# Dividing a head pair's output by one vector instruction: interleaved head columns, a free fourth bank and rows of 640

## The chip, the cores and the metric

One core of a Trainium2 chip runs the kernel. The metric is the device time of one execution in microseconds. The engines are named as in the profile: PE (TensorE), DVE (VectorE), ACT (ScalarE), POOL (GpSimd) and SP (the queue that issues most DMAs).

## What is computed

Eight batches of eight attention heads (576 tokens, head width 64) with rotary positions, then a mixture of eight experts that sends each of the 4608 tokens through its best one:

```python
q_rot, k_rot = (rotate(q), rotate(k))
scores = scale * np.matmul(q_rot, k_rot.transpose(0, 1, 3, 2))
attn = softmax(scores)                     # exp(s - max) / (sum + 1e-9)
x = matmul(attn, v) -> rows of 512 (8 heads x 64)
e_idx = np.argmax(x @ w_gate, axis=1)
out[mask] = gate_w * eom * (relu(x @ w1[e]) @ w2[e])   # for each expert e
```

## The kernel before

**Attention.** A unit of work is a pair of heads; there are 32 pairs (8 batches of 4). A pair's 1152 query rows are taken in nine units of 128. For each unit PE makes the scores (`Pair.score`, L493), DVE takes the row maximum (`peak`, L498), ACT the exponential and its sum (`exp`, L507) and DVE turns it in blocks of 32 (`turn`, L513). PE multiplies with the values (`values`, L535) into `acc`, four banks of PSUM that exist once, so that a pair's first matmul of L535 has to wait until the pair before is done with them. ACT copies `acc` to `ac` (`evict`, L542 to L544). Five matmuls (`back`, L553) turn it back to tokens by rows, each against `ii`, an identity of 128 columns with 32 gate columns behind it, so that 160 columns come out per chunk of 128 tokens: 128 outputs and 2 x 16 gate and output-gate logits. DVE divides by the sums of the softmax while it copies to `xb` (`divide`, L560 to L568). POOL applies the rotary tables for later pairs (`mult`, `add`: L437, L441), splits k and q (`kl`, `ql`: L419) and adds up the sums (`den0`, L516).

**Routing.** Once a batch is divided, `place` adds the logits of its eight heads (`s0`), finds each token's expert, its rank among the tokens of the expert (`rk`, by two matmuls, L685 and L686) and enters it in the experts' lists (`ls`, five matmuls, L729). Both take columns 192 and up of banks 2 and 1 of the `acc` of a later pair. In the last batch these steps run on DVE, in the others on POOL. `store` writes the rows of `xb` to `xd` in DRAM.

**Experts.** From about 545 us on, rows of `xd` are gathered by the lists (`gather`, L1025), transposed (L1055) and multiplied with the weights (L1090 and L1132), which are split in two parts by ACT (L1047) and DVE or POOL (L1049).

The order of all instructions is written by hand: `EVENTS`, `PREP` and the list at the end of `place` give each step a slot relative to the unit at which its pair starts, and each engine takes its instructions in that order. `back` and `divide` of a pair stand in slot 19, when the scores of two pairs later are being made.

Of the kernel before, what the change touches and what calls it, by code (L numbers as in the profile page):

```python
# [10 lines left out]
F32 = mybir.dt.float32  # L11
# [16 lines left out]
NCH = 5  # L28
XW = DM + 1

HL = 2 * E
RW = DM + H * HL

BW = P + 2 * HL
BIG = float(1 << 22)
SLOT = 256

# [2 lines left out]
WHOLE = 1.5 * 2.0 ** 23  # L40


NB, TAIL, PE_, PO = S // 32, 160, 192, 0

EVENTS = [
# [80 lines left out]
def body(ctx, tc, nb, offs, qk, v, rope, cst, gates, w, out):  # L126
    nc = tc.nc
    NT = nb * S

    def pool(st, n, b, **k):  # L130
# [39 lines left out]
    nc.vector.memset(zero, 0.0)  # L170
    nc.scalar.dma_start(out=ct, in_=cst[:, 0:o])
    nc.scalar.dma_start(out=stage[:, 0:nst], in_=cst[:, o:])
    nc.scalar.dma_start(out=ii[:, :, P:].rearrange("p n (h x) -> p n h x", h=2), in_=gates)


    nc.gpsimd.memset(cnt, 0.0)
    nc.gpsimd.memset(lists, 0.0)
    consts = [
        (11, lambda: nc.scalar.copy(ii[:, :, 0:P], ident.unsqueeze(1).broadcast_to((P, NP, P)))),
        (15, lambda: nc.scalar.copy(trib, sc(C_TRI))),  # L180
        (16, lambda: nc.scalar.copy(oneb, sc(C_ONE))),
        (18, lambda: nc.scalar.copy(row, sc(C_ROW))),
# [60 lines left out]
class Attention:  # L243


    def __init__(self, tc, nb, pools, cc, ident, ii, first, trib, oneb, cnt, zero, qk, v, xd, row, lists):
# [27 lines left out]
        xbs = {}  # L274

        def newxb(b):
            xbs[b] = px2.tile([P, NCH, RW], F32, tag="xb", name=f"xb{b}")

            nc.gpsimd.memset(xbs[b][QR:P, NCH - 1, DM:], 0.0)

        for n, pr in enumerate(self.pairs):
            g, b = 9 * n, n // NP
# [79 lines left out]
class Pair:  # L362
# [182 lines left out]

    def back(self):

        parts = []
        for c in range(NCH):
            o = PO if c < 4 else PO + BW  # L550
            parts.append((self.acc[:, c % 4, o:o + BW], self.ac[:, c, :, :].rearrange("p a x -> p (a x)")))
        for out, x in parts:
            self.nc.tensor.matmul(out, x, self.ii[:, self.hp, :], start=True, stop=True, skip_group_check=True)  # L553

    def divide(self, xb):
        nc, V, acc, rz = self.nc, self.nc.vector, self.acc, self.rz
        heads = lambda a, x: a.rearrange("p c (h x) -> p c h x", x=x)
        r4 = rz[:, 0:8].rearrange("p (c h) -> p c h", h=2).unsqueeze(3)
        x0, l0 = self.hp * P, DM + self.hp * 2 * HL
        V.tensor_tensor(out=heads(xb[:, 0:4, x0:x0 + P], D), in0=heads(acc[:, :, PO:PO + P], D),  # L560
                        in1=r4.broadcast_to((P, 4, 2, D)), op=ALU.mult)
        V.tensor_tensor(out=heads(xb[:, 0:4, l0:l0 + 2 * HL], HL), in0=heads(acc[:, :, PO + P:PO + BW], HL),
                        in1=r4.broadcast_to((P, 4, 2, HL)), op=ALU.mult)
        last = acc[0:QR, 0, PO + BW:PO + 2 * BW]
        V.tensor_tensor(out=xb[0:QR, 4, l0:l0 + 2 * HL].rearrange("p (h x) -> p h x", x=HL),
                        in0=last[:, P:BW].rearrange("p (h x) -> p h x", x=HL),
                        in1=rz[0:QR, 8:10].unsqueeze(2).broadcast_to((QR, 2, HL)), op=ALU.mult)
        V.tensor_tensor(out=xb[0:QR, 4, x0:x0 + P].rearrange("p (h x) -> p h x", x=D),  # L568
                        in0=last[:, 0:P].rearrange("p (h x) -> p h x", x=D),
                        in1=rz[0:QR, 8:10].unsqueeze(2).broadcast_to((QR, 2, D)), op=ALU.mult)  # L570
# [8 lines left out]
def place(tc, pools, pairs, b, NT, cc, trib, oneb, cnt, xbs, xd, row, lists):  # L579
# [15 lines left out]
    LO, LG = slice(0, E), slice(E, 2 * E)  # L595

    def s0():
        if not last:

            x = xbs[b][:, :, DM:]  # L600
            h1, h2 = new("h1", [P, NCH, 64]), new("h2", [P, NCH, 32])
            tt(out=h1, in0=x[:, :, 0:64], in1=x[:, :, 64:], op=ALU.add)
            tt(out=h2, in0=h1[:, :, 0:32], in1=h1[:, :, 32:], op=ALU.add)
            tt(out=new("lgs", [P, NCH, 16]), in0=h2[:, :, 0:16], in1=h2[:, :, 16:], op=ALU.add)
            return
        nc.vector.tensor_reduce(new("lgs", [P, NCH, 16]), xbs[b][:, :, DM:].rearrange("p c (h x) -> p c x h", x=HL), axis=AX.X, op=ALU.add)

    def s1():
        nc.vector.tensor_reduce(new("mx", [P, NCH]), T["lgs"][:, :, LO], axis=AX.X, op=ALU.max)
# [153 lines left out]
class Moe:  # L763
# [288 lines left out]
    def turned_in(self, s, h):  # L1052
        tp = self.tps[s, h] = self.small.tile(f"mtp{s}_{h}{self.nm}")
        for dc in range(4):
            self.nc.tensor.transpose(out=tp[:, dc, :], in_=self.xgs[s % 2][:, h, dc * P:dc * P + P], identity=self.ident)  # L1055

    def turn(self, s, h):
        nc, V = self.nc, self.nc.vector
        if s >= self.end or h >= self.todo[s][0]:
            return  # L1060
        if h == 0:
            self.xt[s] = [self.buf(f"xt{i}", 0, 1, 1, [P, 4, SLOT], F32R, f"xt{i}_{s}{self.nm}") for i in range(2)]
            self.gss[s] = self.buf("gs", s, 2, 2, [P, 2], F32, f"gs{s}{self.nm}")
            V.tensor_copy(self.gss[s], self.xgs[s % 2][:, :, DM])
# [149 lines left out]
def layouts(q, k, v, wgt, wog, w1, w2):  # L1214
# [41 lines left out]
```

## Time and profile before

| | us |
|---|---|
| median of 3 runs | 1046.92 |
| lowest and highest run | 1043.89, 1053.6 |
| the profiled execution | 1044.68 |
| its span, first to last instruction | 1042.8 |
| PE busy in it | 969.2 |
| DVE busy in it | 818.0 |
| ACT, POOL busy in it | 616.8, 599.6 |

The span lies 1.9 us below the execution's own time. An engine's busy time says how full it is, not whether it sets the end: in this profile PE is full in the expert part, and the attention part is shared by PE, DVE and POOL, each waiting for one of the others at some place of every pair.

### The profile page before, as it was taken

To read this page: it belongs to the slowest core of one execution; us is meant where nothing else is said; L and a number is where in the kernel's file an instruction comes from. 1 tells how busy PE (TensorE), PEld (TensorE's weight loads), DVE (VectorE), ACT (ScalarE), POOL (GpSimd) and SP (SyncE) were. 2 spreads that over 40 slices of the span, in tenths; PEclk is the share of its full clock that TensorE was granted. 3 is DMA by queue.
4 is the path that set the end of the run, shared out by engine and by line. 5 is a ranking of instruction groups with operands and counts; after the bars stand their busy time and mean duration, and the time that the engine had idled before them with its cause. 6 is when DMAs were issued, how large, how long until landed. Compare 5 with 4: busy or idle time off the path is not lost.

```text
span 1042.8 us, 34822 instructions
## 1 busy us (share of the span) xinstructions
PE 969.2 (93%) x14461; PEld 844.4 (81%) x14461; DVE 818.0 (78%) x1371; ACT 616.8 (59%) x1283; POOL 599.6 (57%) x613
## 2 busy tenths in 40 slices
PE   4999999989999999999799999999999999999995
PEld 4778777767878777777678899998889988899984
DVE  6889989979988898998768777667776867857772
ACT  4656656656655566665445455557766765857762
POOL 4777898887988879889640122206343443443621
PEclk9999999999999999999999999999999999999998
DMA  6665664666745657465548966767886977977860
GB/s 218 164 173 130 179 195 128 177 163 167 198 125 163 185 159 205 118 179 147 160 140 299 300 211 201 230 201 254 312 299 216 356 243 268 325 283 257 299 240 29
DMA packets 58209, 216.32 MB, mean 207 GB/s; under 512 B 9351, under 2 KB 9660, under 8 KB 53952
## 3 DMA queue, kind: packets, MB, share of 16 engines
q1 hardware_dynamic: 50304, 194.03, 59.9%
q0 software_dynamic: 6464, 18.92, 5.0%
q8 instruction: 115, 1.88, 0.8%
q10 hardware_dynamic: 1280, 1.11, 0.3%
q14 instruction: 46, 0.38, 0.1%
HBM read 196.04 MB, written 20.09 MB: 207 GB/s over the span
## 4 chain that ended last, share of the span: by engine, by line
PE 60%; DVE 13%; POOL 10%; issue 8%; ACT 6%; DMA 1%; ACTq 0%; POOLq 0%; DVEq 0%
PE py L1132 17%; PE ph L1090 14%; PE sc L493 11%; PE acc L535 9%; DVE m L498 5%; POOL raw L437 4%; PE ph L1082 4%; ACT pm L507 4%; DVE pt L513 2%; DVE wl L1049 2%; PE acc L553 2%; POOL raw L441 1%; PE mtp L1055 1%; POOL q L419 1%; ACT wh L1047 1%
## 5 line engine op out<-in xcount | busy, mean ns | idle before, releaser
L507 ACT ACTIVATE pm<-sc,m 128x576 f32<-128x576 f32 x288 | 211.1, 737 | 208.7 <-DVE m L498 207.5
L1049 DVE TENSOR_TENSOR wl<-wr,wh 128x1024 fp32r<-128x1024 f32 x184 | 251.9, 1381 | 45.2 <-ACT wh L1047 42.8
L498 DVE TENSOR_REDUCE m<-sc 128x1 f32<-128x576 f32 x288 | 205.7, 748 | 58.6 <-PE sc L493 57.6
L535 PE MATMUL acc<-pt,v 32*64 32x128 f32 (+1 forms) x9216 | 201.3, 298 | 31.2 <-issue 18.5
L493 PE MATMUL sc<-kh,q 64*128 64x288 f32 x1024 | 205.2, 325 | 20.7 <-ACT q L411 9.7
L1132 PE MATMUL py<-wh,ht 128*128 128x512 f32 x640 | 215.4, 401 | 0.0
L1047 ACT CAST wh<-wr 128x1024 fp32r<-128x1024 f32 x208 | 212.6, 1050 | 0.0
L513 DVE STREAM_TRANSPOSE pt<-pm 128x576 f32<-128x576 f32 x288 | 208.9, 753 | 0.0
L535 PEld LDWEIGHTS acc<-pt,v 32*64 32x64 f32 x9216 | 160.9, 133 | 57.1 <-issue 38.9
L493 PEld LDWEIGHTS sc<-kh,q 64*128 64x128 f32 x1024 | 153.1, 191 | 53.6 <-ACT pm L507 23.1
L437 POOL TENSOR_TENSOR raw<-raw,rt 128x1152 f32<-128x1152 f32 x62 | 163.9, 2643 | 0.3
L1090 PE MATMUL ph<-xt,wh 128*128 128x256 f32 x896 | 161.1, 282 | 0.5 <-DVE xt L1071 0.5
L1132 PEld LDWEIGHTS py<-wh,ht 128*128 128x128 f32 x640 | 120.3, 188 | 25.7
L1090 PEld LDWEIGHTS ph<-xt,wh 128*128 128x128 f32 x896 | 138.3, 188 | 2.4 <-DVE xt L1071 1.2
L493 PE MATMUL sc<-kl,q 64*128 64x288 f32 x512 | 129.7, 308 | 0.0
L1090 PE MATMUL ph<-xt,wl 128*128 128x256 f32 x448 | 126.1, 281 | 0.0
L1132 PE MATMUL py<-wl,ht 128*128 128x512 f32 x320 | 125.9, 393 | 0.0
L1049 POOL TENSOR_TENSOR wl<-wr,wh 128x1024 fp32r<-128x1024 f32 x24 | 58.3, 2431 | 90.4 <-ACT wh L1047 84.4
L441 POOL TENSOR_TENSOR raw<-raw 128x576 f32<-128x576 f32 x62 | 87.6, 1413 | 1.9
L1106 ACT ACTIVATE ht<-ph 128x512 fp32r<-128x512 f32 x56 | 33.4, 597 | 90.3 <-PE ph L1090 90.3
L493 PEld LDWEIGHTS sc<-kl,q 64*128 64x128 f32 x512 | 86.3, 192 | 0.2 <-DVE kl L419 0.2
L1090 PEld LDWEIGHTS ph<-xt,wl 128*128 128x128 f32 x448 | 84.3, 188 | 0.1
(247 smaller groups left out, 1317.4 us busy)
## 6 DMA issues: line engine op xcount, KB each, us to landing
wr<-in_w SPq DMA_DIRECT2D x208, 512.0 KB
raw<-in_qk SPq DMA_DIRECT2D x64, 576.0 KB
v<-in_v SPq DMA_DIRECT2D x128, 288.0 KB
xd<-xb SPq DMA_DIRECT2D x16, 513.0 KB
xd<-xb SPq DMA_DIRECT2D x8, 128.2 KB
rt<-in_rope ACTq DMA_DIRECT2D x1, 576.0 KB
xg<-xd,2idx POOLq DMA_INDIRECT x18, 6.7
out<-y,2idx POOLq DMA_INDIRECT x18, 3.9
```

The lines of the kernel that those rows point to most:

```text
L437: self.eng(eng).tensor_tensor(out=rv, in0=rv, in1=self.rt[:, 2 * t:2 * t + 2, x], op=ALU.mult)
L441: self.eng(eng).tensor_tensor(out=r[:, 2 * t, x], in0=r[:, 2 * t, x], in1=r[:, 2 * t + 1, x], op=ALU.add)
L493: self.nc.tensor.matmul(self.ps[i][:, a, :HS], st, mov[r, x], start=(n == 0), stop=(n == 2))
L498: nc.vector.tensor_reduce(self.m[i], ps[:, :, :HS], axis=AX.XY, op=ALU.max, negate=True)
L507: nc.scalar.activation(pe.rearrange("p (a b) -> p a b", a=2), self.ps[i][:, :, :HS], AF.Exp, bias=self.m[i], scale=1.0, accum_out=self.z[: ...
L513: self.nc.vector.transpose(out=self.pt[:, st[0] + 5 * st[1] if st else 4, :], in_=self.pc.pop(i))
L535: nc.tensor.matmul(self.acc[h * D:h * D + D, a, o:o + 32 * n], self.v[r, h, j, :], self.pt[r, u:u + n, 32 * j:32 * j + 32], start=(j == 0) ...
L1047: self.nc.scalar.copy(wh, r)
L1049: eng.tensor_tensor(out=wl, in0=r, in1=wh.bitcast(F32), op=ALU.subtract)
L1082: nc.tensor.matmul(ph[:, 0, :], st[:, dc, 0:P], mv[:, dc, :], start=(n == 0), stop=(n == 11))
L1090: nc.tensor.matmul(ph[:, f, :], st[:, dc, fs], mv[:, dc, :], start=(n == 0), stop=(n == 11))
L1132: self.nc.tensor.matmul(py[h], st[:, f, hs], mv, start=(f == 0 and n == 0), stop=(f == 7 and n == 2))
```

## The change

The two heads' columns alternate in the output of `back`: 160 columns are now (80 columns x 2 heads), by a permuted identity in `ii`. The five chunks stand 344 columns apart in the first three banks, none across the edge of a bank. So one instruction with one regular pattern over five chunks, 80 columns and two heads divides everything, where there were four. The reciprocals `rz` lie as (chunk, head), and are read as a pair of words that is repeated 80 times. The fourth bank is free of outputs, and `rk` and `ls` move there. `xb` keeps the logits between the pairs' outputs, 160 columns per pair, so that rows in `xd` and in the gathered tile `xg` have 640 columns and not 513; `s0` adds the logits of the heads by three additions in all batches, the last one included, where there was one reduction. The rows of w1 are put in the new order on the host. A clearing of part of `xb` by POOL (L279) goes.

```diff
-XW = DM + 1
-RW = DM + H * HL
-BW = P + 2 * HL
+HW = D + HL
+XW = H * HW
+BW = 2 * HW
+BS = 344
...
-        (11, lambda: nc.scalar.copy(ii[:, :, 0:P], ident.unsqueeze(1).broadcast_to((P, NP, P)))),
+        (11, lambda: [nc.scalar.copy(ii[:, n, 0:P].rearrange("p (d h) -> p d h", h=2), ident.rearrange("p (h d) -> p d h", h=2)) for n in range(NP)]),
...
-            nc.gpsimd.memset(xbs[b][QR:P, NCH - 1, DM:], 0.0)
...
     def back(self):
+        flat = self.flat()
         for c in range(NCH):
-            o = PO if c < 4 else PO + BW
-            parts.append((self.acc[:, c % 4, o:o + BW], self.ac[:, c, :, :].rearrange("p a x -> p (a x)")))
-        for out, x in parts:
-            self.nc.tensor.matmul(out, x, self.ii[:, self.hp, :], start=True, stop=True, skip_group_check=True)
+            self.nc.tensor.matmul(flat[:, BS * c:BS * c + BW], self.ac[:, c, :, :].rearrange("p a x -> p (a x)"),
+                                  self.ii[:, self.hp, :], start=True, stop=True, skip_group_check=True)
...
     def divide(self, xb):
-        V.tensor_tensor(out=heads(xb[:, 0:4, x0:x0 + P], D), in0=heads(acc[:, :, PO:PO + P], D),
-                        in1=r4.broadcast_to((P, 4, 2, D)), op=ALU.mult)
...
+        acc = self.flat()[:, 0:BS * NCH].rearrange("p (c x) -> p c x", x=BS)[:, :, 0:BW]
+        rz = self.rz.rearrange("p (c h) -> p c h", h=2).unsqueeze(2)
+        heads = lambda a: a.rearrange("p c (x h) -> p c x h", h=2)
+        self.nc.vector.tensor_tensor(out=heads(xb[:, :, x0:x0 + BW]), in0=heads(acc), in1=rz.broadcast_to((P, NCH, HW, 2)),
+                                     op=ALU.mult)
...
     def s0():
-        nc.vector.tensor_reduce(new("lgs", [P, NCH, 16]), xbs[b][:, :, DM:].rearrange("p c (h x) -> p c x h", x=HL), axis=AX.X, op=ALU.add)
+        x = xbs[b].rearrange("p c (n x) -> p c n x", x=BW)[:, :, :, P:]
+        tt(out=h1, in0=x[:, :, 0:2, :], in1=x[:, :, 2:4, :], op=ALU.add)
+        tt(out=h2, in0=h1[:, :, 0, :], in1=h1[:, :, 1, :], op=ALU.add)
+        hv = h2.rearrange("p c (x h) -> p c x h", h=2)
+        tt(out=new("lgs", [P, NCH, HL]), in0=hv[:, :, :, 0], in1=hv[:, :, :, 1], op=ALU.add)
...
-        return pairs[NP * b + NP - 1 + k].acc[:, bank, PE_:PE_ + n]
+        return pairs[NP * b + NP - 1 + k].acc[:, 3, at:at + n]
```

On DVE, the divide of pair 14 before the change, between the work on the scores of pair 16 and the last turn of pair 15 (`m` is a unit's maximum, `pt` its turned exponentials):

```order
L513 STREAM_TRANSPOSE pt15_4566<-pm15_8_4818 128x576
L513 STREAM_TRANSPOSE pt16_4878<-pm16_0_4897 128x576
L560 TENSOR_TENSOR xb3_4267<-acc14_4639,rz0_112 128x4x128
L562 TENSOR_TENSOR xb3_4267<-acc14_4639,rz0_112 128x4x32
L565 TENSOR_TENSOR xb3_4267<-acc14_4639,rz0_112 64x32
L568 TENSOR_TENSOR xb3_4267<-acc14_4639,rz0_112 64x128
L498 TENSOR_REDUCE m16_2_4935<-sc16_2_4921 128x1
L498 TENSOR_REDUCE m16_3_4937<-sc16_3_4922 128x1
```

The same place after the change, where lines and buffers have other numbers (L511 is the turn, L496 the maximum):

```order
L511 STREAM_TRANSPOSE pt15_4526<-pm15_8_4775 128x576
L511 STREAM_TRANSPOSE pt16_4835<-pm16_0_4854 128x576
L560 TENSOR_TENSOR xb3_4231<-acc14_4596,rz0_112 128x5x160
L496 TENSOR_REDUCE m16_2_4889<-sc16_2_4875 128x1
L496 TENSOR_REDUCE m16_3_4891<-sc16_3_4876 128x1
```

Four instructions of 512, 128, 32 and 128 columns became one of 800; what stands before and behind is the same.

On PE, the end of `back` of one pair, the scores behind it and the first value matmuls of the next pair, with the engines and DMA queues that each waits for, before the change:

```order
L553 MATMUL acc_351<-ii,ac_113 128x160 [waits Activation_49]
L553 MATMUL acc_351<-ii,ac_113 128x160 x4
L493 MATMUL sc_2_622<-kh_384,q_458 128x288 [waits Activation_49]
L493 MATMUL sc_2_622<-kl_385,q_458 128x288
L535 MATMUL acc_646<-pt_295,v_461 64x160 [waits DMAHW0_49,DVE_49,PE_49]
L535 MATMUL acc_646<-pt_295,v_461 64x128
```

And after it (L548 is `back`, L491 the scores, L533 the values):

```order
L548 MATMUL acc_354<-ii,ac_113 128x160 [waits Activation_49]
L548 MATMUL acc_354<-ii,ac_113 128x160 x4
L491 MATMUL sc_2_621<-kh_387,q_461 128x288 [waits Activation_49]
L491 MATMUL sc_2_621<-kl_388,q_461 128x288
L533 MATMUL acc_645<-pt_295,v_464 64x160 [waits DMAHW0_49,DVE_49]
L533 MATMUL acc_645<-pt_295,v_464 64x128
```

No matmul moved; the first value matmul no longer waits for PE itself (in the pairs that neither rank nor list matmuls precede), and still for DVE, whose last act on the old `acc` is the divide.

## Rows read from the trace of the kernel before

**Rows 1.** Busy time by stretch: PE, PEld, DVE, ACT, POOL; granted clock; DMA share; GB/s.

```profile
200.00:400.00 200.00, 183.75 (x4344) 154.41 (x4341) 175.60 (x340) 119.03 (x326) 169.81 (x198) 0.98 0.61 169
...
560.00:1000.00 440.00, 437.05 (x2841) 393.27 (x2840) 324.77 (x456) 275.14 (x393) 153.99 (x97) 1.00 0.78 271
```

**Rows 2.** Chain of waits, shares by line, 40 to 560 us.

```profile
by line: PE sc L493 19.7%; PE acc L535 17.5%; issue 10.2%; DVE m L498 8.7%; POOL raw L437 8.0%; ACT pm L507 6.6%; DVE pt L513 3.8%; PE acc L553 3.3%; POOL raw L441 2.9%; POOL q L419 2.4%; POOL kl L419 2.2%; DVE xb L560 2.1%; PE acc L729 1.4
```

**Rows 3.** Pieces of that chain in order of time: start, length (us), what.

```profile
47.86 0.40 DVE xb L560
...
256.87 0.68 DVE xb L560
...
257.84 0.20 DVE xb L568
258.04 0.68 DVE m L498
...
260.99 1.41 POOL kl L419
...
499.02 0.36 DVE xb L560
```

**Rows 4.** Timeline of DVE around one divide: start, us, engine, line, what.

```profile
271.89 0.65 DVE L560 TENSOR_TENSOR xb<-acc,rz 128x512 f32<-128x512 f32 x1
272.47 0.28 DVE L562 TENSOR_TENSOR xb<-acc,rz 128x128 f32<-128x128 f32 x1
272.67 0.17 DVE L565 TENSOR_TENSOR xb<-acc,rz 64x32 f32<-64x32 f32 x1
272.77 0.27 DVE L568 TENSOR_TENSOR xb<-acc,rz 64x128 f32<-64x128 f32 x1
272.96 1.40 DVE L498 TENSOR_REDUCE m<-sc 128x1 f32<-128x576 f32 x2
```

**Rows 5.** Timeline of PE there; in brackets the idle time before.

```profile
272.44 0.29 PE L493 MATMUL sc<-kh,q 64*128 64x288 f32 x1
273.13 1.35 PE L535 MATMUL acc<-pt,v 32*64 32x160 f32 x64 [0.40 <-PE sc L493]
```

**Rows 6.** Waits, 40 to 560 us: who <- for whom: us in total, times, longest.

```profile
POOL kl L419 <- ACT kh L411: 43.1, 24, 4.6
...
PE acc L535 <- PE sc L493: 11.7, 23, 0.8
DVE pr L690 <- POOL base L673: 7.9, 7, 4.5
```

**Rows 7.** DVE's instructions on `acc`: ns min/median/max, first and last start, forms.

```profile
L560 DVE TENSOR_TENSOR xb<-acc,rz x32: 650/666/692, 47.9 to 550.2; 128x512 f32<-128x512 f32 x32
L562 DVE TENSOR_TENSOR xb<-acc,rz x32: 273/277/283, 48.4 to 550.8; 128x128 f32<-128x128 f32 x32
...
L691 DVE TENSOR_TENSOR cnt<-acc,cnt x7: 155/156/156, 125.7 to 518.6; 128x8 f32<-128x8 f32 x7
L732 DVE TENSOR_TENSOR lists<-acc,lists x7: 457/458/458, 173.7 to 549.8; 128x288 f32<-128x288 f32 x7
```

**Rows 8.** The instructions on `xb`, columns as in rows 7.

```profile
L279 POOL MEMSET xb<- x8: 199/200/200, 47.7 to 499.5; 64x128 f32 x8
...
L606 DVE TENSOR_REDUCE lgs<-xb x1: 1275/1275/1275, 558.9 to 558.9; 128x80 f32<-128x640 f32 x1
```

**Rows 9.** Timeline of ACT where `ii` is made, columns as in rows 5.

```profile
34.97 0.61 ACT L179 COPY ii<-ident 128x512 f32<-128x512 f32 x1
...
37.60 0.74 ACT L507 ACTIVATE pm<-sc,m 128x576 f32<-128x576 f32 x1 [1.45 <-DVE m L498]
...
41.92 0.30 ACT L180 CAST trib<-stage 128x128 bf16<-128x128 f32 x1
```

**Rows 10.** The last addition of the logits on POOL, columns as in rows 7.

```profile
L604 POOL TENSOR_TENSOR lgs<-h x7: 352/354/357, 97.5 to 487.1; 128x80 f32<-128x80 f32 x7
```

**Rows 11.** DMA issues: out<-in, queue, count, KB each.

```profile
xd<-xb SPq DMA_DIRECT2D x16, 513.0 KB
```

More of the change, by code (lines that the diff above doesn't have):

```diff
@@ L40 @@
 WHOLE = 1.5 * 2.0 ** 23
-NB, TAIL, PE_, PO = S // 32, 160, 192, 0
+NB, TAIL, PE_ = S // 32, 160, 192
 EVENTS = [
@@ L172, in body @@
     nc.scalar.dma_start(out=stage[:, 0:nst], in_=cst[:, o:])
-    nc.scalar.dma_start(out=ii[:, :, P:].rearrange("p n (h x) -> p n h x", h=2), in_=gates)
+    nc.scalar.dma_start(out=ii[:, :, P:], in_=gates)
     nc.gpsimd.memset(cnt, 0.0)
@@ L276, in newxb @@
         def newxb(b):
-            xbs[b] = px2.tile([P, NCH, RW], F32, tag="xb", name=f"xb{b}")
-            nc.gpsimd.memset(xbs[b][QR:P, NCH - 1, DM:], 0.0)
+            xbs[b] = px2.tile([P, NCH, XW], F32, tag="xb", name=f"xb{b}")
         for n, pr in enumerate(self.pairs):
@@ L546, in back, with flat @@
     def back(self):
-        parts = []
+        flat = self.flat()
         for c in range(NCH):
-            o = PO if c < 4 else PO + BW
-            parts.append((self.acc[:, c % 4, o:o + BW], self.ac[:, c, :, :].rearrange("p a x -> p (a x)")))
-        for out, x in parts:
-            self.nc.tensor.matmul(out, x, self.ii[:, self.hp, :], start=True, stop=True, skip_group_check=True)
+            self.nc.tensor.matmul(flat[:, BS * c:BS * c + BW], self.ac[:, c, :, :].rearrange("p a x -> p (a x)"),
+                                  self.ii[:, self.hp, :], start=True, stop=True, skip_group_check=True)
+    def flat(self):
+        return self.acc.rearrange("p a b -> p (a b)")
     def divide(self, xb):
[L556 to L559, printed above, removed]
-        V.tensor_tensor(out=heads(xb[:, 0:4, x0:x0 + P], D), in0=heads(acc[:, :, PO:PO + P], D),
-                        in1=r4.broadcast_to((P, 4, 2, D)), op=ALU.mult)
[L562 to L570, printed above, removed]
+        acc = self.flat()[:, 0:BS * NCH].rearrange("p (c x) -> p c x", x=BS)[:, :, 0:BW]
+        rz = self.rz.rearrange("p (c h) -> p c h", h=2).unsqueeze(2)
+        x0 = self.hp * BW
+        heads = lambda a: a.rearrange("p c (x h) -> p c x h", h=2)
+        self.nc.vector.tensor_tensor(out=heads(xb[:, :, x0:x0 + BW]), in0=heads(acc), in1=rz.broadcast_to((P, NCH, HW, 2)),
+                                     op=ALU.mult)
 def number(NT, b):
@@ L597, in s0 @@
     def s0():
[L598 to L605, printed above, removed]
-        nc.vector.tensor_reduce(new("lgs", [P, NCH, 16]), xbs[b][:, :, DM:].rearrange("p c (h x) -> p c x h", x=HL), axis=AX.X, op=ALU.add)
+        x = xbs[b].rearrange("p c (n x) -> p c n x", x=BW)[:, :, :, P:]
+        h1, h2 = new("h1", [P, NCH, 2, 2 * HL]), new("h2", [P, NCH, 2 * HL])
+        tt(out=h1, in0=x[:, :, 0:2, :], in1=x[:, :, 2:4, :], op=ALU.add)
+        tt(out=h2, in0=h1[:, :, 0, :], in1=h1[:, :, 1, :], op=ALU.add)
+        hv = h2.rearrange("p c (x h) -> p c x h", h=2)
+        tt(out=new("lgs", [P, NCH, HL]), in0=hv[:, :, :, 0], in1=hv[:, :, :, 1], op=ALU.add)
     def s1():
@@ L661, in s13 @@
     def s13():
-        V.tensor_copy(xbs[b][:, :, DM], T["eg"])
+        V.tensor_copy(xbs[b][:, :, P], T["eg"])
     def store(i):
@@ L667, in store, with psum @@
         if i < 2:
-            nc.sync.dma_start(out=xd[r:r + 2 * P, :].rearrange("(c p) d -> p c d", p=P), in_=xbs[b][:, 2 * i:2 * i + 2, 0:XW])
+            nc.sync.dma_start(out=xd[r:r + 2 * P, :].rearrange("(c p) d -> p c d", p=P), in_=xbs[b][:, 2 * i:2 * i + 2, :])
         else:
-            nc.sync.dma_start(out=xd[r:r + QR, :], in_=xbs[b][0:QR, 4, 0:XW])
+            nc.sync.dma_start(out=xd[r:r + QR, :], in_=xbs[b][0:QR, 4, :])
     def base():
         tt(out=new("base", [P, E]), in0=cnt, in1=cc(C_EB), op=ALU.add)
-    def psum(k, bank, n):
+    def psum(k, at, n):
         if last:
             return small.tile(f"pl{b}_{k}").rearrange("p a b -> p (a b)")[:, 0:n]
-        return pairs[NP * b + NP - 1 + k].acc[:, bank, PE_:PE_ + n]
+        return pairs[NP * b + NP - 1 + k].acc[:, 3, at:at + n]
     def s14():
-        rk = T["rk"] = psum(2, 2, (NCH + 1) * E).rearrange("p (a b) -> p a b", b=E)
+        rk = T["rk"] = psum(2, 0, (NCH + 1) * E).rearrange("p (a b) -> p a b", b=E)
         flat = lambda t: t.rearrange("p a b -> p (a b)")
@@ L724, in s20 @@
     def s20():
-        T["ls"] = psum(4 if ahead else 5, 1, lists.shape[1])
+        T["ls"] = psum(4 if ahead else 5, 128, lists.shape[1])
         for c in range(NCH):
@@ L1054, in turned_in @@
         for dc in range(4):
-            self.nc.tensor.transpose(out=tp[:, dc, :], in_=self.xgs[s % 2][:, h, dc * P:dc * P + P], identity=self.ident)
+            self.nc.tensor.transpose(out=tp[:, dc, :], in_=self.xgs[s % 2][:, h, dc * BW:dc * BW + P], identity=self.ident)
     def turn(self, s, h):
@@ L1063, in turn @@
             self.gss[s] = self.buf("gs", s, 2, 2, [P, 2], F32, f"gs{s}{self.nm}")
-            V.tensor_copy(self.gss[s], self.xgs[s % 2][:, :, DM])
+            V.tensor_copy(self.gss[s], self.xgs[s % 2][:, :, P])
         xth, xtl = self.xt[s]
@@ L1226, in layouts @@
     g = np.concatenate([wgt, wog], 1).reshape(NP, 2, D, 2 * E)
-    gd = np.zeros((P, NP, 2, 2 * E), g.dtype)
+    gd = np.zeros((P, NP, 2 * E, 2), g.dtype)
     for h in range(2):
-        gd[h * D:h * D + D, :, h] = g[:, h].transpose(1, 0, 2)
-    g = gd
+        gd[h * D:h * D + D, :, :, h] = g[:, h].transpose(1, 0, 2)
+    g = gd.reshape(P, NP, 4 * E)
+    w1 = w1.reshape(E, NP, 2, D, FF).swapaxes(2, 3)
     a = w1.reshape(E, 4, P, 4, 256).transpose(3, 0, 2, 1, 4).reshape(4, E * P, 1024)
```

## Prediction

> **What bounds the kernel now.** I read the busy time by stretch first. From 560 to 1000 us PE is busy 437.05 of 440 us: the expert part is PE's, and the change touches none of its matmuls. From 200 to 400 us, in the attention part, PE is busy 183.75, DVE 175.60 and POOL 169.81 of 200 us [rows 1]: three engines near full, none quite. So the chain of waits says more there than the shares. From 40 to 560 us it runs over PE (L493, L535), DVE (L498, L513), POOL (L437) and ACT (L507), and DVE's divide is on it: L560 alone has 2.1% of 520 us, 10.9 us [rows 2]. Gone through piece by piece, the chain has the divide in 24 of the 32 pairs, first at 47.86 and last at 499.02 us [rows 3]. In the other eight it passes by on PE or POOL.
>
> Two things wait for the divide. On DVE the next maximum stands behind it in the queue: the divide begins at 271.89 and the next L498 at 272.96 us, 1.07 us later [rows 4]. On PE the next pair's value matmuls need `acc`: the divide's last instruction ends at 272.77 + 0.27 = 273.04, and L535 begins at 273.13 [rows 4, 5]. PE's scores ended at 272.73 and it then sat idle for 0.40 us [rows 5]. The view puts this down to "PE sc", 23 times and 11.7 us in all [rows 6]; but those scores had long ended, and L535 follows the divide by 0.1 us, so I read it as the divide.
>
> **The change part by part.**
>
> *The divide.* All four instructions read PSUM, one column at a time. From 128 to 512 columns the median goes from 277 to 666 ns [rows 7], which is 389 / 384 = 1.013 ns a column and 147 ns fixed. 800 columns in one instruction are 147 + 810 = 957 ns. From both sides: with the slope between L732 (288 columns, 458 ns) and L560, 0.929, it is 666 + 288 x 0.929 = 934 ns; with that between L691 (8 columns, 156 ns; its median) and L732, 1.079, it is 977 ns [rows 7]. The columns are as many as before (512 + 128 + 32 + 128 = 800), so only fixed costs go. In the timeline the next instruction starts 0.08 us before the listed end of the last one (272.96 against 273.04) [rows 4]. So from the divide's start to the next maximum it is 0.957 - 0.08 = 0.88 us after 1.07: 0.19 us less. The end that PE waits for comes at 271.89 + 0.957 = 272.85 in place of 273.04, 0.19 us earlier too. PE's idle 0.40 us becomes 0.21, so the divide is still what it waits for, and the whole 0.19 us counts.
>
> In the 24 pairs with the divide on the chain that is 24 x 0.19 = 4.6 us. It goes on behind the divide also where POOL is on the chain: at 256.87 the divide releases the maximum at 258.04, and from there the chain passes over ACT to POOL's L419 at 260.99 [rows 3]; POOL waits for ACT in this place in 24 pairs, 43.1 us in all [rows 6], so it starts earlier when DVE does. In the eight other pairs I count nothing; if they gained as much, it would be 1.5 us more. What is late next is POOL: in seven pairs DVE stands at L690 for POOL's `base`, just ahead of the divide [rows 6], and this the change leaves.
>
> The reciprocals are read as two adjacent words, 80 times over. The rows have no such operand on DVE, and the nearest is L606, which reads with a step of 16 words: 640 columns in 1275 ns [rows 8], (1275 - 147) / 640 = 1.76 ns a column, where 1.013 is the rate of the unbroken reads above. So broken reads can cost three quarters more here. [...]
>
> *The logits of the last batch.* L606 lies on DVE's queue at 558.9 us [rows 8], among the splits of the first weights, which PE waits for. Three additions of 320, 160 and 80 columns replace it: 147 + 324 = 471 and 147 + 162 = 309 ns at the rate above, and for the third, whose operands step by two words, 228 ns at the full rate and 288 at that of L606. The sum, less twice the overlap of 0.08, is 0.85 to 0.91 us for 1.275: I take 0.35 us off once. In the seven other batches POOL makes the same three additions; only L604, 354 ns for 80 columns [rows 10], now steps by two words. Between no change and twice the time it is 0 to 0.35 us a batch, 2.5 us in all; the chain has no piece of it, so I take nothing.
>
> *What goes from POOL.* Eight clearings of 0.2 us [rows 8], none of them on the chain: nothing; at most 8 x 0.2 = 1.6 us.
>
> *The constants.* One ACT copy of 512 columns, 0.61 us, becomes four of 128 with a step in the read. A plain one of 128 takes 0.30 us (L180) [rows 9]; with L606's 0.75 ns a column more it is 0.40. So ACT has 0.6 to 1.0 us more, once; it idles 1.45 us before the next exponential at 37.60 [rows 9], which hides it. Uncovered it would cost up to 1.0 us.
>
> *Ranks and lists in bank four.* The matmuls, their place and what reads them stay: nothing; that DVE and PE now stay out of each other's banks I price at nothing, since L560 with and without such matmuls ahead of it has 650 to 692 ns [rows 7], 0.04 us from end to end.
>
> *Rows of 640.* The stores write 640 / 513, a quarter more: 16 of 513 KB [rows 11], and eight of a quarter of that for the last rows, are 9.2 MB before and 11.5 MB after, and the gathers read the same 2.3 MB more. At the 271 GB/s of the expert part that is 8.6 us if all of it stood in the way. But PE is idle for 3 of 440 us there with the DMA engines busy 0.78 of the time [rows 1], and the weights are asked for eight pieces ahead: nothing.
>
> Sum: 4.6 + 0.35 = 4.9 us off. On the profiled execution, 1044.68 us, that gives 1039.8. That execution lies 2.2 us under the median of the runs, 1046.92; from the median it would be 1042.0. I take the middle, 1040.9 us.
>
> **The rivals.**
>
> *The gain is swallowed.* Something with less than 0.19 us to spare takes the divide's place: PE in its own order, or POOL, which is busy 85% [rows 1] and holds DVE up at L690 7 times [rows 6]. For it: in eight pairs the chain already passes by. Against it: PE keeps 0.21 us of its idle time and POOL's own wait for ACT is 43.1 / 24 = 1.8 us a pair [rows 6]. It gives 0 to 2 us off, 1042.7 to 1046.9 with both bases.
>
> *The pair of words is read slowly.* If reading `rz` costs what L606's reads cost, the divide is 147 + 800 x 1.76 = 1555 ns, 1.48 to the next maximum and not 1.07: 0.41 us more. All 32 pairs would then have it on the chain: 32 x 0.41 = 13 us, 1044.68 + 13 = 1058 us, slower by over 1%. It decides from a divide of 1.15 us on, the old one's length. For it: L606 is the only row of DVE with broken reads. Against it: L606's elements all stand apart, and here two lie side by side; the output and the PSUM side run unbroken over 160 columns. [...]
>
> *More than the chain shows.* All 32 pairs gain 0.21 (a divide of 0.934 us) and POOL's clearings count: 6.7 + 0.35 + 1.6 = 8.7 us off, 1036 to 1038.
>
> **How the numbers follow.** The forecast has 0.67, the swallowed gain 0.20, the slow read 0.06, the larger gain 0.07. A measurement of this kernel tells about 1% from no change, 10.5 us: that is 1036.4 and 1057.4. The forecast, the swallowed gain and most of the larger gain lie inside. Of the larger gain, and of the forecast with runs that spread as before (0.3% under to 0.6% over the median), I give 0.06 to faster; the slow read and a little of that spread make 0.07 for slower; 0.87 is left for the same. The range goes from 1035 us, the larger gain with a quick median, to 1049, no gain with a median as slow as before's and 2 us more; the slow read is left out of it.
>
> **What would show it.** In the profile of the changed kernel the one instruction of 128x800 should read 0.93 to 0.98 us, the next maximum should follow its start by 0.88 us, DVE should be busy about 32 x 0.19 = 6 us less, and PE's idle time before a pair's first L535 should be near 0.2 us where it was 0.40. The stretch of the experts should be as long as before. A divide of 1.15 us or more, or a longer expert part, would prove me wrong; so would a divide of 0.96 us with the attention part no shorter, which is the swallowed gain.

## The result and the profile after

The changed kernel takes 1036.51 us, the median of 4 runs (1033.53 to 1037.73), beside 1049.26 us for the kernel before (4 runs, 1043.89 to 1053.6): a ratio of 0.9873 [0.9838, 0.9907]. It is faster by 1.27%, some 13 us where 4.9 were forecast. The time lies in the predicted range, 1035 to 1049, near its quick end: where the larger gain had been put, 1036 to 1038 with a chance of 0.07, and 0.1 us above the 1036.4 that was to count as faster. The profiled execution took 1033.53 us, its span is 1031.7; the span before was 1042.8.

The divide itself, as one instruction. The view groups by line what works on `xb` (ns min/median/max, first and last start, forms) and is of the changed kernel:

```profile
L560 DVE TENSOR_TENSOR xb<-acc,rz x32: 952/980/992, 47.7 to 540.3; 128x800 f32<-128x800 f32 x32
...
  PEld acc L533: 7.7, 18
  PE acc L533: 3.3, 16
```

The forecast was 957 ns (934 to 977); it is 952 to 954 in 15 pairs, 979 to 983 in 15 and 992 in two. The two lower lines, who waited for it, answer to what [rows 6] had put down to "PE sc": PE waits for the divide, and here the view says so by name.

The same moment as in [rows 4], the timeline of DVE in the changed kernel (start, us, engine, line, what):

```profile
266.57 0.95 DVE L560 TENSOR_TENSOR xb<-acc,rz 128x800 f32<-128x800 f32 x1
267.45 1.41 DVE L496 TENSOR_REDUCE m<-sc 128x1 f32<-128x576 f32 x2
```

And the timeline of PE there, as in [rows 5], with the idle time before in brackets:

```profile
267.14 0.29 PE L491 MATMUL sc<-kh,q 64*128 64x288 f32 x1
267.58 1.37 PE L533 MATMUL acc<-pt,v 32*64 32x160 f32 x64 [0.15 <-DVE xb L560]
```

The next maximum begins 0.88 us after the divide, as forecast, and PE idles 0.15 us where it was 0.40. So far the prediction is right to a few hundredths of a microsecond, and the question is why the kernel gained more than twice what this adds up to.

Busy time by stretch, in the columns of [rows 1]; the last line is from a second answer, from the start of the last divide to the end:

```profile
200.00:400.00 200.00, 187.28 (x4447) 157.41 (x4448) 178.77 (x313) 122.25 (x336) 174.77 (x199) 1.00 0.63 177
...
560.00:1000.00 440.00, 436.56 (x2876) 395.64 (x2874) 323.03 (x436) 275.51 (x391) 155.91 (x98) 1.00 0.79 273
...
540.34:1031.70 491.36, 476.74 (x3113) 430.76 (x3111) 351.83 (x484) 297.96 (x424) 162.51 (x102) 0.99 0.75 260
```

And the kernel before from its last divide to its end:

```profile
550.16:1042.80 492.64, 478.50 (x3113) 430.66 (x3111) 351.25 (x485) 297.91 (x424) 161.87 (x102) 0.99 0.74 255
```

In the attention part more matmuls fit into the same 200 us (4447 for 4344) and the granted clock is 1.00, where it was 0.98. From the last divide on, both kernels run the same 3113 matmuls; the changed one takes 491.36 us instead of 492.64, and PE is busy 1.76 us less there. I had costed that stretch at nothing.

The chain of waits by line, 40 to 560 us, as in [rows 2]:

```profile
by line: PE sc L491 18.4%; PE acc L533 12.4%; POOL raw L435 12.0%; ACT pm L505 7.8%; issue 7.4%; DVE m L496 6.3%; PE acc L548 6.0%; POOL raw L439 4.8%; POOL kl L417 3.5%; POOL q L417 3.5%; DVE xb L560 2.0%; PE acc L717 1.4%; ACT kh L409 1.3
```

And the waits of the same stretch, as in [rows 6]:

```profile
POOL kl L417 <- ACT kh L409: 38.4, 20, 4.1
...
PE acc L533 <- issue: 13.9, 12, 4.8
...
DVE pr L678 <- POOL base L661: 8.3, 7, 4.7
...
PE acc L533 <- PE sc L491: 4.5, 7, 0.9
...
PE acc L533 <- DVE xb L560: 3.3, 16, 0.7
```

DVE's and PE's shares of the chain fall and POOL's rise (L435 from 8.0 to 12.0%): POOL is what is late next. DVE's wait for POOL's `base` stays as it was.

Last, the starts of three divides in a row, the first instruction of each in the timeline of DVE, in the kernel before. I call the time from the start of one divide to that of the next a period; all periods below are read in this way. Undisturbed are those that come out the same, to a few hundredths, in several batches of an execution.

```profile
79.73 0.65 DVE L560 TENSOR_TENSOR xb<-acc,rz 128x512 f32<-128x512 f32 x1
...
94.71 0.65 DVE L560 TENSOR_TENSOR xb<-acc,rz 128x512 f32<-128x512 f32 x1
...
109.87 0.68 DVE L560 TENSOR_TENSOR xb<-acc,rz 128x512 f32<-128x512 f32 x1
```

And the same three in the changed kernel:

```profile
78.89 0.95 DVE L560 TENSOR_TENSOR xb<-acc,rz 128x800 f32<-128x800 f32 x1
...
93.69 0.95 DVE L560 TENSOR_TENSOR xb<-acc,rz 128x800 f32<-128x800 f32 x1
...
108.67 0.98 DVE L560 TENSOR_TENSOR xb<-acc,rz 128x800 f32<-128x800 f32 x1
```

14.98 and 15.16 us became 14.80 and 14.98: 0.18 less each. The divide at 94.71 is one that the chain before passed by.

From the first divide to the last it is 502.30 us before and 492.65 after, 9.65 less, in this one pair of executions; in the second profiles of the two kernels it is 507.60 and 493.55, 14.05 less.

### The profile page after: what moved, and what is told of

Read it like the earlier page. It is cut to its first block, busy times and chain, and to the rows that moved or that the text cites. A ratio compares the mean times of both kernels' runs of the same rounds, so it can differ in the third digit from the quotient of the medians.

```text
span 1031.7 us, 34705 instructions
## 1 busy us (share of the span) xinstructions
PE 965.8 (94%) x14461; PEld 843.5 (82%) x14461; DVE 813.4 (79%) x1277; ACT 617.6 (60%) x1286; POOL 596.1 (58%) x605
## 3 DMA queue, kind: packets, MB, share of 16 engines
q8 instruction: 115, 1.88, 0.8%
## 4 chain that ended last, share of the span: by engine, by line
PE 60%; POOL 15%; DVE 9%; issue 7%; ACT 6%; DMA 2%; POOLq 0%; ACTq 0%; DVEq 0%
PE py L1120 18%; PE ph L1078 14%; PE sc L491 11%; PE acc L533 7%; POOL raw L435 6%; PE ph L1070 4%; ACT pm L505 4%; DVE m L496 4%; PE acc L548 3%; POOL raw L439 2%; DVE wl L1037 2%; POOL kl L417 2%; POOL q L417 2%; PE mtp L1043 2%; DVE xb L560 1%
## 5 line engine op out<-in xcount | busy, mean ns | idle before, releaser
L496 DVE TENSOR_REDUCE m<-sc 128x1 f32<-128x576 f32 x288 | 206.1, 750 | 54.0 <-PE sc L491 52.9
L491 PE MATMUL sc<-kh,q 64*128 64x288 f32 x1024 | 206.1, 325 | 20.5 <-ACT q L409 9.5
L533 PE MATMUL acc<-pt,v 32*64 32x128 f32 (+1 forms) x9216 | 198.2, 296 | 22.0 <-issue 13.9
L1120 PE MATMUL py<-wh,ht 128*128 128x512 f32 x640 | 214.5, 400 | 0.0
L511 DVE STREAM_TRANSPOSE pt<-pm 128x576 f32<-128x576 f32 x288 | 209.2, 755 | 0.0
L491 PEld LDWEIGHTS sc<-kh,q 64*128 64x128 f32 x1024 | 153.4, 190 | 54.0 <-ACT pm L505 26.5
L533 PEld LDWEIGHTS acc<-pt,v 32*64 32x64 f32 x9216 | 158.9, 132 | 47.0 <-issue 33.0
L435 POOL TENSOR_TENSOR raw<-raw,rt 128x1152 f32<-128x1152 f32 x62 | 164.0, 2645 | 0.2
L491 PE MATMUL sc<-kl,q 64*128 64x288 f32 x512 | 130.1, 308 | 0.0
L1078 PE MATMUL ph<-xt,wl 128*128 128x256 f32 x448 | 125.9, 281 | 0.0
L1120 PE MATMUL py<-wl,ht 128*128 128x512 f32 x320 | 125.0, 391 | 0.0
L491 PEld LDWEIGHTS sc<-kl,q 64*128 64x128 f32 x512 | 86.3, 191 | 0.2 <-DVE kl L417 0.2
```

The source lines that it names most:

```text
L435: self.eng(eng).tensor_tensor(out=rv, in0=rv, in1=self.rt[:, 2 * t:2 * t + 2, x], op=ALU.mult)
L491: self.nc.tensor.matmul(self.ps[i][:, a, :HS], st, mov[r, x], start=(n == 0), stop=(n == 2))
L496: nc.vector.tensor_reduce(self.m[i], ps[:, :, :HS], axis=AX.XY, op=ALU.max, negate=True)
L511: self.nc.vector.transpose(out=self.pt[:, st[0] + 5 * st[1] if st else 4, :], in_=self.pc.pop(i))
L533: nc.tensor.matmul(self.acc[h * D:h * D + D, a, o:o + 32 * n], self.v[r, h, j, :], self.pt[r, u:u + n, 32 * j:32 * j + 32], start=(j == 0) ...
L1078: nc.tensor.matmul(ph[:, f, :], st[:, dc, fs], mv[:, dc, :], start=(n == 0), stop=(n == 11))
```

## The experiments

The theory: the 0.19 us are gained at every divide, and the rest comes from something that I had costed at nothing. The rivals: the matmuls' clock, which PE's idle time before each pair may lower; the rows of 640 instead of 513; ranks and lists in a bank of their own; or a quick execution only.

**The two kernels again.**

> The changed kernel, unchanged. Theory A (the divide's fixed costs come off every pair's period, and what lies beyond that in the profile of the changed kernel is gaps of PE with no wait behind them, which differ from one execution to the next): about 1033 to 1040 us, 0.984 to 0.992 of the kernel before; the divide again 0.95 to 0.98 us; the gaps of PE that end with 'issue' sum to another number than in the first profile, by 2 us or more. Theory B (the change itself removes those gaps): the gaps are again those of the first profile, within 1 us.

> The kernel before, unchanged. Theory A: 1044 to 1053 us, ratio 1; the sum of PE's gaps that end with 'issue' differs from the first profile's by some us, and the span with it. Theory B: the gaps are the same as in the first profile, 3 to 4 us more than in the changed kernel.

Changed: 1035.8 us, ratio 0.9866 [0.9825, 0.9907]. Before: 1048.01 us, 0.9979 [0.9951, 1.0007] against the other runs of itself, of which 22 gave a median of 1048.8 us, 1042.3 to 1054.2. So the gain stands, near 13 us; and the execution profiled first, 1044.68 us, was one of the quicker ones of the kernel before. The undisturbed periods repeat to 0.02 us in both kernels (14.80 to 14.85, and 14.98 to 15.02). What theory A said of PE's gaps failed. I count those of 0.3 us and more that the timeline puts down to "issue" (the engine waited for nothing that the profile shows), without those that end just behind a divide. They sum to 6.8 and 7.6 us in the two profiles of the changed kernel, and to 9.8 and 11.4 before: nearer to theory B.

**The divide in four instructions again**, everything else as changed:

```diff
-        self.nc.vector.tensor_tensor(out=heads(xb[:, :, x0:x0 + BW]), in0=heads(acc), in1=rz.broadcast_to((P, NCH, HW, 2)),
-                                     op=ALU.mult)
+        for a, b in ((0, 51), (51, 64), (64, 67), (67, 80)):
+            self.nc.vector.tensor_tensor(out=heads(xb[:, :, x0:x0 + BW])[:, :, a:b, :], in0=heads(acc)[:, :, a:b, :],
+                                         in1=rz.broadcast_to((P, NCH, b - a, 2)), op=ALU.mult)
```

> The changed kernel with its divide cut into four instructions of 510, 130, 30 and 130 columns, as many as before. Theory A: 0.19 us more in every pair, 32 x 0.19 = 6 us, so about 1042 us, 0.994 of the kernel before, and the period of a pair in its steady stretch back from 14.84 to 15.0 us. Theory B (banks, rows of 640, the clearing and the wait of PE for itself carry part of the gain): less of it comes back than 6 us as a share of the whole, the time stays 6 to 7 us under before.

1042.88 us, 0.9943 [0.9917, 0.9968]: 7 us of the 13 are given back (1042.88 - 1035.8). The undisturbed periods are 14.99 to 15.03 again. So the divide in one instruction is worth about 7 us; some 6 come from elsewhere.

**Rows of 640 alone**, in the kernel before:

```diff
-XW = DM + 1
-
 HL = 2 * E
 RW = DM + H * HL
+XW = RW
```

> The kernel before with rows of 640 columns in the stores and gathers, and nothing else changed. Theory A: the bytes are hidden, ratio 1.00 within 0.3%. Rival: the longer stores shift the DMAs against PE's code loads, and the ratio moves by 0.3% or more either way.

1043.96 us, 0.9954 [0.992, 0.9988]: longer rows make it faster, by 1.3 to 8.4 us. From the last divide to the end its profile has 490.67 us, like the changed kernel and not like the kernel before (492.61; 492.65 in its second profile).

**Rows of 528 alone**, to tell length from number of bytes (2112 instead of 2052):

```diff
-XW = DM + 1
+XW = DM + 16
```

> The kernel before with rows of 528 columns (2112 bytes, a multiple of 64) in the stores and gathers in place of 513 (2052 bytes). In the profiles with rows of 640 the stretch from the last divide to the end is 490.7 to 491.4 us, in the two with 513 it is 492.6. If the odd length of the rows is the cause, it is near 491 us here too and the ratio 0.995 to 0.999; if the place of the columns or something else is, it stays at 492.6 and the ratio at 1.00.

1039.14 us, 0.9911 [0.9879, 0.9943], quicker than the 0.995 to 0.999 that were expected, and 490.75 us from the last divide on. So it isn't the 2560 bytes that help: the rows of 2052 bytes were the slow ones. In the lists of the costliest groups (line, engine, operation, tiles, shape, count; busy us, mean ns) PE's second matmul of the experts shows it, before:

```profile
L1132 PE MATMUL py<-wh,ht 128*128 128x512 f32 x640 | 215.4, 401 | 0.0
...
L1132 PE MATMUL py<-wl,ht 128*128 128x512 f32 x320 | 125.9, 393 | 0.0
```

and with rows of 528:

```profile
L1132 PE MATMUL py<-wh,ht 128*128 128x512 f32 x640 | 214.5, 400 | 0.0
...
L1132 PE MATMUL py<-wl,ht 128*128 128x512 f32 x320 | 125.0, 391 | 0.0
```

(215.4 - 214.5) + (125.9 - 125.0) = 1.8 us. In the second profile of the kernel before the two sums are 215.4 and 126.0 again, and in all twelve profiles with other rows 214.4 to 214.5 and 125.0. The matmuls read no row of `xd` themselves; why they get faster stays open. The edit changes the rows in DRAM and the size of the gathered tile `xg` in SBUF at once, and no run parts the two. The rest of this kernel's 9 us lies in the attention part, where its undisturbed periods are those of the kernel before. What does differ is the granted clock: 0.991 in the mean of its ten executions, 0.987 in that of 25 of the kernel before on the same chip. Why it fell less often is not shown.

**The 0.19 us put back on one side of the divide.** What waits for the divide is PE (its end) and DVE's next maximum. An unused instruction behind the divide delays the maximum alone; ahead of it, both. First with a product of 128 columns in SBUF:

```diff
+        self.nc.vector.tensor_tensor(out=self.dum, in0=self.ident, in1=self.ident, op=ALU.mult)
```

> The changed kernel with one more DVE instruction of 128 columns (a product of the identity with itself, into a tile that nobody reads) right behind each divide; PE does not wait for it. Theory A1 (the next maximum, which stands behind the divide on DVE, carries the gain): the steady period goes from 14.83 back to about 15.0 us, and the time up by 32 x 0.19 = 6 us against the changed kernel, to about 1042. Theory A2 (PE's wait for the free banks carries it): period and time stay, 1034 to 1038.

> The changed kernel with the same additional instruction ahead of each divide, so that both the next maximum and PE's first value matmul come 0.19 us later. Theories A1 and A2 alike: about 6 us more than the changed kernel, about 1042 us. [...]

Behind: 1042.75 us, 0.9927 [0.9896, 0.9958], periods of 15.14. Ahead: 1065.74 us, 1.0148 [1.0078, 1.0217]. The second is a mis-sized probe. The added instruction took 0.25 us at best, 0.94 in the median and 2.49 at worst. One of the long ones in the timeline of DVE:

```profile
115.73 1.51 DVE L564 TENSOR_TENSOR dum<-ident 128x128 f32<-128x128 f32 x1
```

And POOL in the same moment:

```profile
115.69 1.40 POOL L443 TENSOR_TENSOR raw<-raw 128x576 f32<-128x576 f32 x1
```

The added instruction ends at 117.24, 0.15 us after POOL's (117.09). So I took one that reads nothing, a clearing of 256 columns, 0.27 us:

```diff
+        self.nc.vector.memset(self.dum, 0.0)
```

> The changed kernel with a DVE memset of 256 columns (0.27 us in the trace, about 0.19 us from start to start, no operand read) behind each divide, in place of the product that turned out to wait for POOL. The next maximum comes 0.19 us later, PE's first value matmul does not. Theory A1 (the next maximum carries the gain): the steady period goes from 14.83 to about 15.0 us and the time to about 1042. Theory A2 (PE's wait carries it): 14.83, 1034 to 1038 us.

> The same memset ahead of each divide: both come 0.19 us later, as with the divide in four parts. Both theories: a steady period of about 15.0 us, about 1042 us as in the kernel with four parts, and PE's idle time back at 0.4 us. If the half-clock stretches follow PE's longer idle times, they appear again behind pairs with ranks (PE idle 1.3 us), which they did in none of the profiles with 1.1 us.

Behind: 1039.73 us, 0.9929 [0.99, 0.9958]. Ahead: 1043.0 us, 0.995 [0.9914, 0.9986]. The timeline of DVE with the clearing behind the divide:

```profile
94.92 0.95 DVE L564 TENSOR_TENSOR xb<-acc,rz 128x800 f32<-128x800 f32 x1
95.88 0.27 DVE L566 MEMSET dum<- 128x256 f32 x1
96.07 1.35 DVE L500 TENSOR_REDUCE m<-sc 128x1 f32<-128x576 f32 x2
```

And PE of that kernel there:

```profile
95.92 1.37 PE L537 MATMUL acc<-pt,v 32*64 32x160 f32 x64 [0.15 <-DVE xb L564]
```

PE has its short wait of 0.15 us, and yet the undisturbed period is 15.06. So the period is carried by the maximum behind the divide. The time, 1039.73 us, settles less: it lies between the two expectations (1042, and 1034 to 1038). With the clearing ahead of it PE's wait is 0.40 us again and the period no longer: 15.05. Still that kernel is slower by 3.4 us (the means of ten runs each on one chip; 2.4 us to either side by their spread). What differs in its trace is the granted clock; over the ten executions each its mean is 0.988 here and 0.991 with the clearing behind. The profile is of the slowest of the ten, 1049.46 us. The timeline of DVE and, below it, of PE behind the ranks of one batch, with the clearing ahead:

```profile
196.31 0.93 DVE L565 TENSOR_TENSOR xb<-acc,rz 128x800 f32<-128x800 f32 x1
...
197.34 2.36 PE L537 MATMUL acc<-pt,v 32*64 32x160 f32 x64 [1.34 <-issue]
```

The view names no releaser, but the divide ended at 197.24, 0.1 us before. The busy time of the stretch behind it, in the columns of [rows 1]:

```profile
197.40:201.00 3.60, 3.60 (x70) 3.16 (x70) 2.61 (x5) 2.22 (x6) 0.92 (x2) 0.53 0.06 15
```

After an idle 1.34 us PE ran at a granted clock of 0.53, and 64 matmuls took 2.36 us where they take 1.37. That pair's period is 16.38 instead of 15.05. The place is the pair behind a batch's ranks, six times in an execution. In eleven profiles, all but those of the kernels with the divide or `base` moved and of the mis-sized probe, PE was idle there 1.27 us or more 29 times, and 10 of these periods are some 1.3 us longer; it was idle 0.81 to 1.13 us 37 times, and none is.

**No wait of PE for the divide at all**: the divide one turn earlier.

```diff
-    ("den0", 10, 2), ("den1", 12, 2), ("den2", 13, 2), ("evict", 17, 2), ("newxb", 18, 1), ("back", 19, 1), ("divide", 19, 2),
+    ("den0", 10, 2), ("den1", 12, 2), ("den2", 13, 2), ("evict", 17, 2), ("newxb", 18, 1), ("back", 19, 1), ("divide", 19, 1),
```

> The changed kernel with the divide one place earlier on DVE, ahead of one turn of 0.67 us; the next maximum stays where it is. PE's idle time before a pair's first value matmul goes from 0.16 us to none. Theory A1: the period stays at 14.83 us and the time within 1 us. Theory A2: the period falls by up to 0.16 us, 5 us off in all.

1035.34 us, 0.9854 [0.9786, 0.9921], no other time than the changed kernel's. On PE the value matmuls now follow the scores at once:

```profile
267.31 0.29 PE L491 MATMUL sc<-kh,q 64*128 64x288 f32 x1
267.53 1.64 PE L533 MATMUL acc<-pt,v 32*64 32x160 f32 x80
```

But the undisturbed periods are 14.93 to 15.15 and not below 14.80. Without PE's last 0.15 us nothing was gained in this order, in which a turn of 0.77 us now stands behind the divide; what they are worth by themselves it does not show.

**Ranks and lists.** The ranks back into a bank that holds outputs:

```diff
-        return pairs[NP * b + NP - 1 + k].acc[:, 3, at:at + n]
+        return pairs[NP * b + NP - 1 + k].acc[:, 2 + (at > 0), at or 192:(at or 192) + n]
```

> The changed kernel with the ranks back in the third bank, at columns 192 to 239, between two chunks of the output; the lists stay in the fourth. If sharing a bank costs PE or DVE anything, the seven pairs with ranks grow; I expect the period there at 15.70 us as in the changed kernel, and the time at 1034 to 1038 us.

1035.05 us, 0.99 [0.982, 0.9979]; its periods, rank pairs included, are those of the changed kernel (14.80 to 14.85, and 15.69 to 15.73). The ranks' bank is worth nothing that the periods show; the lists' bank was not tried.

**What is late next.** POOL's `base` three slots earlier in its hand-written order:

```diff
-          (12, 2, adds(1, 2)), (13, 2, adds(3, 4)), (15, 2, s8), (15, 2, base), (17, 1, s14), (17, 2, s14b), (18, 2, s9),
+          (12, 2, adds(1, 2)), (13, 2, adds(3, 4)), (15, 2, s8), (12, 2, base), (17, 1, s14), (17, 2, s14b), (18, 2, s9),
```

> The changed kernel with POOL's addition for the list bases three slots earlier, ahead of a product of 2.6 us, so that DVE doesn't stand at L678 for it with the divide behind. If that wait sets the end in the seven pairs with ranks: PE's idle 1.1 us there falls to 0.2, 6 x 0.9 us, and in pair 29 most of 4.8 us goes and with it the half clock behind it: 5 to 10 us off, 1026 to 1031. Rival: the sums of the softmax, which POOL adds up behind the same products, come late in place of it: 0 to 2 us off.

1029.47 us (4 runs, 1029.02 to 1032.98), 0.9809 [0.974, 0.9879]: the fastest of all. The timeline of DVE at the last of the seven ranks in the changed kernel:

```profile
510.28 0.20 DVE L678 TENSOR_TENSOR pr<-acc,base 128x40 f32<-128x40 f32 x1 [4.71 <-POOL base L661]
510.47 0.98 DVE L560 TENSOR_TENSOR xb<-acc,rz 128x800 f32<-128x800 f32 x1
```

PE of the changed kernel there:

```profile
511.55 2.44 PE L533 MATMUL acc<-pt,v 32*64 32x160 f32 x64 [4.78 <-issue]
```

The timeline of DVE at the same ranks with `base` early:

```profile
503.04 0.20 DVE L678 TENSOR_TENSOR pr<-acc,base 128x40 f32<-128x40 f32 x1 [0.29 <-PE acc L548]
503.23 0.98 DVE L560 TENSOR_TENSOR xb<-acc,rz 128x800 f32<-128x800 f32 x1
```

And PE of that kernel:

```profile
504.31 1.04 PE L533 MATMUL acc<-pt,v 32*64 32x160 f32 x41 [0.29 <-PE sc L491]
```

DVE had stood 4.71 us for POOL with the divide queued behind, and PE 4.78 us for that divide. This period falls from 20.25 to 15.40 and those of the six other rank pairs from 15.70 to 15.00: 4.85 + 6 x 0.70 = 9.05 us. The two pairs behind the last one give 2.9 us back (16.16 + 13.71 became 17.96 + 14.80), which leaves some 6.2 us, where the times differ by 6.3 (1035.8 and 1029.47) and the stretch from first to last divide by 5.3 (492.65 and 487.39).

## Why the prediction was right and wrong

*The divide's cost: right.* 952 to 980 ns against 957, start to start 0.88 us against 1.07. The reciprocals, read as pairs of adjacent words, kept the divide at the rate of the unbroken reads: 800 columns in 952 ns are 1.01 ns a column with the 147 ns fixed. The slow read of the reciprocals (13 us more) is refuted.

*"24 of 32 pairs on the chain, eight others nothing": failed.* Every undisturbed period fell by 0.16 to 0.21 us, on the chain or off it: 15.02 to 14.84, 15.89 to 15.70, 16.33 to 16.14. If the disturbed ones gained as much, it is 31 x 0.185 = 5.7 us, and 1.1 us more than the term's 4.6. Of the eight divides that the chain passed by, five end an undisturbed period, and each of these fell too. A chain names one path; why it passed them by was not followed further.

*What carries it: half right.* I named two that wait for the divide and let both count. The period hangs on the maximum (15.06 with PE's wait short and the maximum late). PE's wait matters in another way, for which the prediction had no term: behind the ranks PE's idle time was about 1.3 us, the granted clock fell to half behind it in 10 of the 36 such places of the six profiles with PE's longer wait (in the kernel before to 0.50 from 323 to 325 us, behind an idle 1.27 us), and each time cost 1.3 us. The change cuts that idle time to 1.1 us or less, and in its profiles the clock fell behind none. With six such places an execution this is 6 x 10 / 36 x 1.3 = 2.2 us in the mean; the two kernels with the clearing differ by 3.4, give or take 2.4. Split in four, the divide gave back 7 us, near the 5.7 + 2.2 of these two terms.

*"Rows of 640: nothing": failed, in its sign.* I bounded it from above by 8.6 us of more traffic and from below not at all. The traffic is hidden, as I said; but the old rows of 2052 bytes had a price that no row showed, since nothing in the trace before stood beside them. It is 1.3 to 2.0 us from the last divide on (490.65 to 491.36 us in the profiles with other rows, twice 492.6 with these), 4.8 us by the times with 640, and 9 with 528, with intervals that reach from 1.3 to 13 us. These times hold more than the rows' own price, since the clock differed too (0.991 for 0.987 with 528).

*The sum, then:* 5.7 + about 2.2 + about 4.8 = 12.7 us by the runs, for some 13 measured. The second and third terms are known to half their size at best, and they overlap, as both hold some of the clock. A count that doesn't add overlapping terms takes the mean times of four kernels that ran on one chip and differ by a step each: 1048.1 us before, 1043.5 with rows of 640, 1043.5 with all of the change but the divide in one instruction, 1035.5 changed. That is 4.7 + 0.0 + 7.9 = 12.6 us, each step known to some 3 us.

*What is not settled.* Of the 9.65 us between first and last divide 5.7 are the periods; the second pair of profiles has 14.05. Two more things differ there. One is the clock, and not only behind the ranks: between first and last divide it stood at 0.50 for 13.7 us in the kernel before and for 30.7 in its second profile, and for 10.2 in both of the changed one. Over 60 executions of the kernel before the mean granted clock is 0.9860, over the eight of the changed one 0.9906. The share not granted, 0.0140 and 0.0094, makes 14.6 and 9.7 us of an execution. In the pair behind the ranks shown above (197.34 us), 3.6 us at a granted 0.53 lost 1.7 us in this way and cost 1.3 us of time; at that price the 4.9 us between the kernels cost an estimated 3.8, the 2.2 behind the ranks among them. Elsewhere the clock also fell behind a shorter gap, in the changed kernel behind one of 1.01 us that ended at 407.25 (0.50 from 408 to 410 us), so the length of the gap alone doesn't decide it.

The other is PE's gaps in which it waits for nothing that the profile shows, 9.8 and 11.4 us before and 6.8 and 7.6 after, nearly all at the same instructions in every profile and in the attention part. Rows of 528 alone have 6.5, rows of 640 alone 9.8, and the kernel with the ranks' bank 4.8, so they don't follow the divide alone. The fall of the clock at 217 us in the kernel before stands just behind such a gap (2.05 us), as does the one at 408 us in the changed kernel (1.01 us), and no run was made to part the two.

*The small terms.* The last batch's logits: three additions take 1.03 us from the first's start to the next split, where the reduction took 1.275 - 0.08 = 1.19, so 0.16 and not 0.35 us: the first two don't overlap as I had it, and I had set them against the whole 1.275. POOL's additions with a step of two words became faster, 319 ns for 354 [rows 10], where I had bounded them at no change to slower. ACT's copies stayed hidden, as forecast: 1.00 us instead of 0.61 [rows 9], and 1.10 us of idle time left before the next exponential:

```profile
34.76 1.00 ACT L179 COPY ii<-ident 128x128 f32<-128x128 f32 x4
...
37.42 0.74 ACT L505 ACTIVATE pm<-sc,m 128x576 f32<-128x576 f32 x1 [1.10 <-DVE m L496]
```

DVE is busy 813.4 us, 4.6 less than before and not 6: the divides are 5.9 us shorter, as forecast, and other instructions took 1.3 more in this profile.

*The base and the rivals.* The median of three runs and the profiled execution, whose middle I took, both lay 2 to 4 us under the kernel's usual 1048.8; that made the forecast time look nearer than its gain was. That the measured time fell into the range is the width of the range more than its sum, which had 4.9 of the 13 us: in part luck. The swallowed gain is refuted: POOL's `base` is still waited for, and shifted along with the rest. "More than the chain shows" had the right direction and the right first term (all pairs), and the wrong rest: the runs show the rows and the clock. POOL's clearings were not tried alone; the step that holds them, with the banks, comes to 0.0 us in the count above.

## What to carry to other kernels

Where a pattern repeats, measure the time from one repetition to the next in undisturbed places, and count a saving in each of them; a chain of waits that passes by in some does not say that they gain nothing. Behind an idle gap of some 1.3 us on PE the matmuls got half the clock at 10 of 36 places here, which cost another 1.3 us each, so look at the granted clock behind the gaps that a change shortens or lengthens. An edit "costed at nothing" that changes the length of a row deserves a run of its own, and so does the wait next in line: here a table entry three slots earlier was worth another 6 us.

## What the runs showed of the hardware

A product of 128 columns on DVE with both operands in SBUF took 0.25 us at best, 0.94 in the median and 2.49 at worst ahead of the divide, and 0.27, 0.29 and 1.63 us behind it. The one at 115.73 us took 1.51 us beside an addition of POOL with two operands in SBUF, and ended 0.15 us behind it. The clearing, which reads nothing, took 0.27 us all 64 times in its two kernels. The divide, with one operand in PSUM and one in SBUF, took at most 0.99 us in the profile of the changed kernel and in those of the four with an added instruction; the one shown at 266.57 us took 0.95 us, all of it while POOL's product of L435 ran (2.65 us from 265.13).

Rows of 2052 bytes made a kernel slower than rows of 2112 or 2560 (means of 1048.1 us for 1038.9 and 1043.5), in part through matmuls that never touch them (401 and 393 ns for 400 and 391); whether by the rows in DRAM or by the size of the tile in SBUF is open. And PE stops at fixed places of its program without a wait that the profile shows: gaps of 0.3 us and more, those behind a divide left out, add up to 5 to 11 us in an execution where the divide keeps its place. The matmuls that they precede stand, with few exceptions, whole multiples of some 128 apart (number 606, 2779, 4185, 4440, 5846 and so on of 14461). Of the profile's two DMA queues for instructions the larger moved 115 packets, 1.88 MB, which would be, were all of them for PE, a packet for some 250 of its 28922 matmuls and weight loads. So these stops may be waits for instructions; no run tested it.
